# Another written order for the first layer and the seam, late weight tiles inside the loop, and the planes of x at a step's end

## The chip, the cores and the metric

The kernel runs on one core of a Trainium2 chip. A core has a matrix engine (TensorE, PE in the profile), three engines for elementwise work (VectorE, DVE; ScalarE, ACT; GpSimd, POOL) and SyncE (SP), which here issues DMAs. Each engine works through its own instructions in order. The metric is the device time of one execution in microseconds; lower is better.

## The reference

Three parts one behind the other: an attention with gates and a running state over 768 steps (2 batches, 8 heads, width 40), and two layers that multiply 1536 tokens of 320 values by gated weights of 1536 columns.

```python
def _attn_ref(q, k, v, i_gate, f_gate, o_gate):
...
    for t in range(S):
...
        m_new = np.maximum(f_gate[:, :, t] + m, i_gate[:, :, t])
        f_stab = np.exp(f_gate[:, :, t] + m - m_new)
        i_stab = np.exp(i_gate[:, :, t] - m_new)
...
        C = f_stab[:, :, None, None] * C + i_stab[:, :, None, None] * np.einsum('bhd,bhe->bhde', vt, kt)
        n = f_stab[:, :, None] * n + i_stab[:, :, None] * kt
        h_tilde = np.einsum('bhde,bhe->bhd', C, qt)
...
        y[:, :, t] = o * h_tilde / denom

def _moe_ref(x, w_gate, w_val, w_out):
    gate = 1.0 / (1.0 + np.exp(-(x @ w_gate)))
    val = x @ w_val
    return (gate * val @ w_out).astype(np.float32)

def _moe2_ref(x, w_gate, w_val, w_out, rms_g):
    rms = np.sqrt(np.mean(x * x, axis=-1, keepdims=True) + 1e-06)
    xn = x / rms * rms_g
    g = xn @ w_gate
    silu = g * (1.0 / (1.0 + np.exp(-g)))
    val = xn @ w_val
    return (silu * val @ w_out).astype(np.float32)
```

## The kernel before

**Numbers.** Everything is fp32. A product of two fp32 operands is made from planes: each operand is split into a rounded high plane and the low rest (`sub`, L138, makes the low plane; `copy`, L245, the high one). A product of x with the weights is a pass of eight matmuls into one PSUM bank (`ORD`), one with `w_out` is three matmuls. Weights come from HBM as tiles f = 0 to b (12 for each layer), 960 KB each, as 64-bit words from which `top_w` (L201, L203) and `mant_w` (L208) join the halves of the fp32 numbers.

**PLAN.** All of the attention, layer 1, the weights of layer 2 and the first five steps of layer 2 are operations with short names. `op(key, fn)` stores each; a written list, `PLAN`, is run through key by key, and each key issues its instructions on whatever engines it uses. `pin` then ties every engine, SP among them, to exactly this order. So a key sets its place on each of its engines, and an instruction that waits holds all those behind it on its engine. The keys, with c a chunk of 256 tokens, f a tile:

- D, E: matmuls on nothing, for an idle TensorE; Fb, F, P, S, K, V, PV, U, I, H, A, O: attention (F is a scan on VectorE, S a product of q and k); X: the result goes to `xT`, transposed, high (XH) and low (XL) plane.
- LW, WT, WM, WO, WG, WR, WL..: load and planes of a layer 1 tile; T, TS, TH, Y: one chunk and tile of layer 1. The last two chunks go together (Tp, Sp, Mp, Hp, Yp).
- LZ (load), ZT (top half: ScalarE for even f, VectorE for odd f), ZM (joined halves), ZG, ZR, ZO (high planes), ZLG, ZLH, ZLR, ZLS, ZOL (low planes): a tile of layer 2. Near the end of PLAN the loads share one buffer: the next one can be issued when the ZM of the last has read it.
- N: the norm. RW, RD, RJ, RH, RL: the first third of x for layer 2: 16-bit planes on GpSimd, a transposing DMA, joined again, high, low.
- Tq (`w_up`, L649; the last digit is the pass), Sq (sigmoid), Mq1 and Mq2 (the two multiplies on VectorE), Hq1 (`fb`, ScalarE), Hq2 (`ft`, GpSimd), Yq (`w_out`, L755): steps 0 to 4 of layer 2. `Mq42` is the second multiply of step 4.

**The loop.** Steps 5 to 35 of layer 2 (12 tiles for each of three groups of 512 tokens) follow in a Python loop. A step i issues, in this order: `r_up(i, 0)`, the second half of `r_out(i-2)`, `r_up(i, 1)` (all matmuls on half the rows, L671, two at a time), sigmoid `w_sg`, multiply `w_m1`, the first half of `r_out(i-1)`, then the work on x for the next group, then `w_m2`, `w_h` (`fb`) and `w_hl` (`ft`). Groups of these matmuls are tied: the first of a group waits for a nop on SP, and that nop waits for the last matmul of the group two before (`behind`, L662). Step 5 has `w_up` in place of `r_up`.

The work on x for the next group is spread over steps by `ev`: four row blocks, one begun per step from step 5 (and 17) on: `d_planes` (GpSimd, two copies, L521, L522), one step later `d_move` (a DMA_TRANSPOSE issued by SP), one later `d_join` (GpSimd, L530) and, at the step's end, `d_h` (ScalarE) and `d_l` (VectorE, which writes the tile the profile calls `wraw`). From the third block on, `d_planes` writes a buffer that a `d_l` has to have read.

Of the kernel before, what the change touches and what calls it, by code (L numbers as in the profile page):

```python
# [51 lines left out]
D0 D1 D2 Lga Gm Gf1 Gi1 Gie D3 Lgr Gf2 Gfe Gmz Gfh Gid Lgs Lqk01 Ltok01 D4 Gt D5 D6 Lqk00 Gse Gms Rm Lms Ltok00 Gfl Gtg O00 O01 Lmr LW0 D7 D8 D9 Fb00
F00 Fb02 D10 Fb03 D11 D12 D13 Fb01 S01 S00 D14 V01 D15 D16 D17 D18 D19 D20 Ri1 K00 F03 F02 F01 P01 Rie V00 PV01 K02 K03 D21 D22 P03 PV03 A01 Rf1 K01
Rf2 U00 Rfe WT0 Lsel P02 P00 H01r H01a Rer H01b LW2 WM0 Rel Rz LW1 Lfd Ltok10 Lqk10 Lf10 Lqg10 Lf11 PV00 WO0 UC00 A03 XR00 UM00 A00 H00r H03r H03a H00a
H00b WT2 Rt2 E0 Rc2 D23 D24 E1 D25 D26 D27 D28 WG0 PV02 XP00 E2 E3 E4 E5 Rg U01 WM2 WO2 LW3 LW4 H03b WR0 WG2 A02 WR2 WLG0 WLG2 H02a H02r WLR2 H02b WLS2
WLR0 WT1 XR01 Rgc UC01 Rt1 Lf12 Rc1 E6 E7 E8 D29 XP01 S10 WM1 WO1 E9 XH01 XH00 XL01 XL00 T02 F10 F11 P10 WLS0 WLH0 T00 Lqg11 Lqk11 Lf13 I10 Ltok11 O10
WG1 WR1 WLR1 TS02 WOH2 TH02 P11 V10 WLG1 K10 WLH1 WLS1 LW5 Lqg20 Lf21 Y020 PV11 LW8 WT3 TS00 WT4 TH00 WM3 IH10 T01 UM01 TS01 WO3 PV10 Y000 Y001 F12 WM4
TH01 H10a Y011 S11 K11 Y021 Y010 WR3 WG3 WLR3 WO4 F13 P13 P12 I11 V11 H10b PV13 PV12 WLG3 WLS3 WLH3 WG4 A10 H10r H10c XR10 WR4 O11 IH11 XP10 H11a A11
XH10 WLH4 WLR4 WOH4 H11r H11b H11c T03 U10 LW9 Lf20 LW6 Lqk20 UC10 WT5 WLS4 WLG4 T04 WO5 TS03 XR11 XP11 TS04 XH11 TH03 XL10 TH040 XL11 WM5 UM10 Y031
I20 Y030 WOH5 WR5 WG5 T11 WOL2 K12 WOL4 F21 TS11 WT8 TH11 T10 TS10 WLH5 K13 WLS5 WLG5 WO8 TH10 WM8 WLR5 T12 Ltok21 Lqg21 WT6 TH041 TH042 LW7 TS12 TH120  # L60
T14 Y040 Y041 WO6 WM6 F20 Y111 Y110 TS14 WG8 TH121 TH122 WR8 T05 WT9 WOH6 WR6 WOH3 WG6 WLR8 TH140 TH141 WOL6 IH20 Y121 Y100 T15 WLH8 WLS8 WLS6 WOL5
WLG6 WLG8 S20 Y101 Lf23 Ltok20 V20 LWa Lf22 Lqk21 LWb TH142 WLH6 K21 TS15 TS05 WT7 TH150 P20 Y120 WO9 TH151 TH050 WLR6 T18 T06 O20 TH051 TH052 TS18 WO7
WM7 P21 U11 UC11 K20 TH152 F22 TH180 F23 PV20 Y140 PV21 Y050 Y141 WG7 TS06 WR7 WLG7 U20 Y151 Y150 T16 Y051 WLS7 WM9 WOH7 TH181 WTa WR9 TH182 UC20 TH060
H20a WTb WOH8 A20 TH061 TS16 TH160 TH161 T13 T08 WLH7 H20r WLR7 WG9 WLG9 K22 WLS9 V21 TH162 Y161 S21 TH062 UM11 TS13 WOL8 WOa Y160 Y180 TH130 WMa WOb
TS08 T07 P23 TH080 WLR9 TH081 I21 T19 TH082 WGa TS07 IH21 WMb WRb P22 TH070 WLGa Y080 Y181 WOL3 WOL7 K23 PV22 Y081 PV23 WGb TH071 WRa WLSa TH072 WLSb
H21a WLRa TS19 TH131 TH132 A21 H21r TH190 Ltok30 Lf31 Lqk30 Lf30 F30 T17 Y061 Y130 T1a Y060 Y070 Y071 S30 Y131 WLGb O21 WOH9 TS17 TH191 WOHa TH192 TS1a
TH170 WOL9 H20b F31 WLRb H21b H21c H20c TH171 WOHb T1b P31 TH172 K30 WOLa WOH0 XR20 WOH1 TH1a0 P30 WOLb TS1b TH1b0 Y191 Y190 XP20 P030 XR21 V30 V030
TH1b1 P031 TH1a1 TH1b2 T09 TH1a2 UM20 Lrms Ltok31 Lf32 Lf40 Lqk31 Lqk41 Lqg30 XP21 T0b Y1b1 F32 P131 XH21 TS09 XH20 XL20 XL21 TH090 Y171 U21 V130 Y1a0
Y1b0 Y170 V230 T23 V31 K31 V330 TS0b TH0b0 P231 N100 TH0b1 O30 TH091 TH0b2 F40 P130 N101 Y1a1 T0a Y0b1 P230 TS23 TH230 TH092 N102 Y090 Y091 Y0b0 UC21
P331 TH231 N110 TS0a WOL0 V031 V131 TH232 UM21 WOL1 TH0a0 P330 TH0a1 TH0a2 N103 T24 PV31 I30 PV30 IH30 H30a N111 N112 N113 A30 Ltok41 T27 U30 Y0a1 Y0a0  # L70
TS24 TH240 UC30 K32 Lf42 S31 TS27 O31 TH241 N000 N010 P32 N011 N012 P032 LZ0 Lf33 ZT0 V231 N001 TH270 F33 T29 T25 P132 P33 H30r TH242 TS25 N013 TH250
N002 P232 TH251 K33 TH252 T20 Y241 Lqg31 T22 Y251 I31 P332 N003 P033 P133 P233 P333 V331 Y230 PV32 Y240 PV33 TS22 IH31 TH220 H30b H30c H31a Lqk40 Lf41
Ltok40 TH271 V40 TH272 F41 K41 Y231 U31 Y250 Y270 Y271 S40 A31 XR30 TH221 K40 H31b TS29 TH290 TH291 UC31 TH292 P40 P41 TS20 P041 Lqg40 Lf43 T28 T21
XP30 V040 P040 H31r P141 TH200 XH30 TH201 H31c V140 TH222 TH202 UM30 XL30 TS28 TH280 TS21 TH210 F42 T2a Y220 Y221 V240 V340 Y200 U40 Y201 UC40 T26 T2b
I40 TH211 P241 P341 P140 TH281 TH212 V41 TH282 P240 TS26 P340 IH40 TH260 Y290 Y291 PV41 PV40 Y210 Y281 XR31 TS2a TH261 TH262 XP31 Y261 V041 V141 TS2b
V241 XH31 UM31 K42 V341 H40a TH2a0 F43 TH2b0 XL31 Y260 Y280 TH2b1 TH2b2 S41 Y211 P43 P42 TH2a1 O40 Lf50 Lqk50 TH2a2 T32 T30 P042 P043 H40b P143 P243
O41 TS30 P142 TS32 P343 Y2b0 Y2b1 Y2a0 Y2a1 T36 Lqg41 I41 Ltok50 Lf51 N200 N210 A40 P242 F51 TH320 TH321 N201 P342 TH300 IH41 Lqg50 K43 UM40 TH322 PV42
PV43 TH301 H41a F50 N211 T31 TH302 V50 A41 TS31 TH310 TH311 TS36 V050 H41r H40r S50 P50 H41b N202 N212 TH312 V150 P51 H40c N203 I50 T38 H41c P051 P050
TH360 T37 Ltok51 Lf52 Lf53 Lqk51 V51 Lqg51 P150 TS37 P250 IH50 P151 N213 T33 Y300 V250 P251 XR41 V350 TH370 Y321 Y301 XP41 Y320 P350 PV50 TH371 TH361
TH362 TH372 TS33 P351 PV51 F52 H50a XH41 V051 F53 A50 H50r TH330 XL41 Y311 T39 Y310 V151 S51 U41 P53 UC41 T3a TS38 TH331 TH332 TS39 V251 XR40 P053 V351  # L80
UM41 P52 XP40 Y331 TH380 TH390 P153 P052 O50 O51 XH40 P152 Y330 T34 H50b XL40 H50c I51 P253 TH381 P353 PV53 P252 P352 PV52 IH51 Y370 Y371 Y361 XW50
TH382 XD50 TH391 TH392 Y360 Y380 Y391 Y381 TS34 H51a H51b A51 H51r H51c XW51 TS3a TH3a0 TH340 TH3a1 XJ50 XH50 TH341 TH3a2 XL50 T35 TS35 TH350 Y3a1 Y390
T3b LZ2 XD51 TH342 XJ51 Y3a0 Y341 Y340 TH351 ZT2 TH352 Y350 TS3b XH51 XL51 ZM0 Tp30 Tp31 TH3b0 TH3b1 TH3b2 Y3b0 N300 Y3b1 Tp00 ZM2 Y351 Sp3 Mp32 Hp31
N310 Sp0 Tp10 RW2 LZ1 RD2 LZ4 ZT4 ZT1 N311 N301 N312 N313 Hp32 ZM1 N302 N303 LZ3 Tp11 Tp01 Tp20 Yp32 Mp02 ZM4 Sp2 Hp01 Hp02 Sp1 Tp21 Tp70 Yp33 Yp02
Yp30 Yp00 Yp01 Yp03 Yp31 RJ2 ZT3 Mp12 Hp11 RH2 ZO0 Mp22 Hp21 ZM3 ZR0 ZG3 RW0 Hp12 Tp71 LZ6 LZb Tp60 Yp13 Yp11 Yp12 Sp7 Mp72 ZTb ZMb Hp22 ZOL0 Yp20 RD0
LZ7 Yp23 Yp21 Yp22 Yp10 Tp50 Tp61 Sp6 ZG0 ZO1 Hp71 ZO3 RJ0 ZLS0 ZLG3 ZOL1 ZOL3 Hp72 ZLH3 Mp62 Tp41 Yp73 ZG1 ZT6 ZR1 RH0 ZO2 ZG2 Sp5 Hp61 ZR2 ZT7 Hp62
Tp90 Tp40 Yp72 Yp71 Tp51 Yp63 Yp61 ZR3 Sp4 ZLR0 ZLR1 ZOL2 ZLG1 ZLG0 Yp60 Yp62 Yp70 ZM6 Mp42 RL2 ZLR2 Mp52 ZLS3 ZLS1 ZLG2 RW1 Tpb0 Tp91 ZM7 ZO6 Hp51
Hp52 ZG7 ZG6 Hp41 Sp9 ZR6 ZR7 ZLS2 ZLG7 Hp42 Mp92 ZLR7 Yp50 Tpb1 Yp41 Yp51 Yp40 Yp52 Yp42 Yp53 Yp43 ZLR6 LZ5 RD1 RL0 ZLR3 Spb ZG4 ZLS6 RJ1 RW3 RD3 RH1
RL1 Mpb2 Tpa0 Hp91 ZO7 Tp80 ZO4 ZOL6 ZLH2 Hp92 ZLG6 ZLS7 Sp8 Hpb1 Hpb2 Spa Tpa1 Tp81 Ypb1 Yp93 Yp91 Mp82 Ypb3 ZT5 Yp92 Yp90 Ypb2 Ypb0 RJ3 RH3 Hp81 ZGb
RL3 ZM5 Mpa2 ZLG4 Tq20 Hpa1 ZO5 ZOb Hp82 LZ8 Tq00 Hpa2 Yp83 Ypa3 ZR4 ZR5 Sq2 N510 ZG5 Sq0 ZT8 Ypa0 Tq01 Ypa2 Yp80 Yp82 Mq21 N511 ZOLb ZOL7 ZLH6 N512  # L90
ZLHb Mq01 N513 Yp81 Tq30 Tq21 Tq10 Ypa1 ZLGb N500 ZLR5 Mq02 N501 N502 N503 Mq22 Hq01 Hq02 Sq3 N400 N401 ZLH7 N402 ZOL5 ZOL4 ZRb N410 N411 N412 Yq02
# [1117 lines left out]
```

## Time and profile before

| | |
|---|---|
| median of 3 runs | 482.18 us (481.48 to 483.06) |
| the profiled execution's own time | 480.16 us |
| its span, first to last instruction | 478.3 us |
| TensorE busy | 457.5 us, 96% |
| VectorE, ScalarE, GpSimd busy | 265.1, 201.0, 232.7 us |
| TensorE's mean granted clock | 0.986 |

The profile's times count from the span's start. In the table, an engine's busy time is the sum over its instructions; what is missing to the span is time in which it waited. Attention and layer 1 fill the first 200 us and overlap with layer 2's first weights behind that; the first matmuls of the loop's tied groups (L671) start at 309.77.

### The profile page before, as it was taken

How to read it: one execution, taken by the hardware profiler on the slowest of the kernel's cores; microseconds unless marked ns; L12 is line 12 of the kernel's file. 1: busy time of each engine (PE TensorE's matmuls, PEld its weight loads, DVE VectorE, ACT ScalarE, POOL GpSimd, SP SyncE). 2: the span in 40 equal slices, each digit the busy share in tenths (PEclk: the TensorE clock that was granted, in tenths of full speed). 3: DMA queues.
4: the chain of work that ended last, by engine and by line, in shares of the span. 5: the costliest groups of instructions: out<-in, count | busy, mean ns of one | idle time of the engine just before them, and what ended most of it. 6: DMA issues, size and time to landing. Idle time of an engine off the chain costs nothing.

```text
span 478.3 us, 9850 instructions
## 1 busy us (share of the span) xinstructions
PE 457.5 (96%) x3915; PEld 411.5 (86%) x3917; DVE 265.1 (55%) x464; ACT 201.0 (42%) x448; POOL 232.7 (49%) x287
## 2 busy tenths in 40 slices
...
GB/s 191 333 325 361 318 172 121 11 148 66 212 39 66 65 147 1 117 198 232 97 100 16 84 1 83 83 20 41 9 57 1 18 34 18 20 38 1 1 1 58
DMA packets 24388, 46.68 MB, mean 98 GB/s; under 512 B 12726, under 2 KB 16198, under 8 KB 24342
## 3 DMA queue, kind: packets, MB, share of 16 engines
...
HBM read 41.24 MB, written 2.05 MB: 90 GB/s over the span
## 4 chain that ended last, share of the span: by engine, by line
PE 87%; DVE 4%; ACT 3%; POOL 2%; DMA 2%; issue 1%; DVEq 0%; ACTq 0%; POOLq 0%; SPq 0%
PE g L597 15%; PE o L671 11%; PE g L671 11%; PE a L671 9%; PE o L630 7%; PE g L649 6%; PE a L649 6%; PE o L755 5%; PE o L597 3%; PE a L340 2%; DMA wraw<-in_w_dram 2%; PE a L432 2%; PE o L627 2%; PE a L430 1%; PE g L602 1%; POOL ft L138 1%
## 5 line engine op out<-in xcount | busy, mean ns | idle before, releaser
L138 POOL TENSOR_TENSOR ft<-p,fb 128x512 fp32r<-128x512 f32 x47 | 61.4, 1308 | 114.2 <-ACT fb L245 113.4
L597 PE MATMUL g<-xT,w 128*128 128x256 f32 x640 | 84.1, 286 | 0.6 <-DVE xT L138 0.6
L597 PEld LDWEIGHTS g<-xT,w 128*128 128x128 f32 x640 | 79.5, 191 | 1.4 <-DVE xT L138 0.8
L671 PE MATMUL a<-xT,w 64*128 64x512 f32 (+1 forms) x310 | 79.8, 385 | 0.0
L671 PE MATMUL g<-xT,w 64*128 64x512 f32 (+1 forms) x310 | 79.8, 385 | 0.0
L239 DVE TENSOR_TENSOR p<-p,g 128x512 f32<-128x512 f32 (+1 forms) x37 | 24.9, 673 | 98.3 <-ACT p L728 96.2
L671 PE MATMUL o<-w,fb 64*128 64x320 f32 (+1 forms) x508 | 57.9, 308 | 12.2 <-ACT fb L245 12.2
L728 ACT ACTIVATE p<-g 128x512 f32<-128x512 f32 x47 | 28.0, 596 | 83.1 <-PE g L671 64.6
L671 PEld LDWEIGHTS o<-w,fb 64*128 64x128 f32 (+1 forms) x508 | 45.5, 187 | 17.3 <-ACT fb L245 12.7
L671 PEld LDWEIGHTS g<-xT,w 64*128 64x128 f32 x310 | 55.0, 187 | 4.0
L671 PEld LDWEIGHTS a<-xT,w 64*128 64x128 f32 x310 | 55.0, 187 | 3.8
L245 ACT ACTIVATE fb<-p 128x512 fp32r<-128x512 f32 (+1 forms) x49 | 30.4, 620 | 58.7 <-DVE p L239 50.8
L138 POOL TENSOR_TENSOR h<-sig,h 128x256 fp32r<-128x256 f32 x42 | 36.2, 866 | 36.4 <-ACT h L245 35.5
L239 DVE TENSOR_TENSOR p<-p,a 128x512 f32<-128x512 f32 (+1 forms) x49 | 33.0, 676 | 27.6 <-ACT p L728 14.7
L630 PE MATMUL o<-w,h 128*128 128x320 f32 x252 | 46.4, 318 | 0.0
L671 PE MATMUL a<-wraw,w 64*128 64x512 f32 (+1 forms) x155 | 44.0, 379 | 0.0
L671 PE MATMUL g<-wraw,w 64*128 64x512 f32 (+1 forms) x155 | 44.0, 379 | 0.0
L671 PE MATMUL o<-w,ft 64*128 64x320 f32 (+1 forms) x254 | 40.5, 313 | 1.9 <-POOL ft L138 1.9
L630 PEld LDWEIGHTS o<-w,h 128*128 128x128 f32 x252 | 37.6, 189 | 1.1 <-POOL h L138 0.5
L138 POOL TENSOR_TENSOR w<-wc,w 128x256 fp32r<-128x256 f32 (+2 forms) x37 | 25.2, 685 | 13.7 <-ACT w L245 8.9
L671 PEld LDWEIGHTS g<-wraw,w 64*128 64x128 f32 x155 | 28.3, 185 | 3.5
L671 PEld LDWEIGHTS a<-wraw,w 64*128 64x128 f32 x155 | 28.3, 185 | 2.3
...
## 6 DMA issues: line engine op xcount, KB each, us to landing
wraw<-in_w_dram SPq DMA_DIRECT2D x24, 959.8 KB, 6.3
...
```

What stands on the lines that cost most here:

```text
L138: eng.tensor_tensor(out=out, in0=a, in1=b, op=ALU.subtract)
L239: eng.tensor_tensor(out=out, in0=a, in1=b, op=op)
L245: a_.activation(out=out, in_=x, func=AF.Copy, scale=scale)
L340: nc.tensor.matmul(out=st[j][:, i * L:(i + 1) * L], lhsT=t[n, 1, i, :], rhs=t[n, 0, i, :], start=True, stop=True)
L432: nc.tensor.matmul(out=ps[:, (o + i) * E:(o + i + 1) * E], lhsT=p[:, i, :], rhs=w[:, o + i, :], start=True, stop=True)
L597: nc.tensor.matmul(out=g[:, m, :], lhsT=w[:, m, ws, :], rhs=x[xs // 3][:, xs % 3, :], start=(i == 0), stop=(i == 7))
L627: nc.tensor.matmul(out=o, lhsT=h[:, b * L:(b + 1) * L], rhs=o32[f], start=(n == 1), stop=(n == NF))
L630: nc.tensor.matmul(out=o, lhsT=h[:, hs, b * L:(b + 1) * L], rhs=wo_t[f][:, ws, :], start=(n == 1 and i == 0), stop=(n == NF and i == 2))
L649: nc.tensor.matmul(out=g, lhsT=w[:, m, ws, :], rhs=x[xs // 3][:, xs % 3, :], start=(i == 0), stop=(i == 7))
L671: k = nc.tensor.matmul(**kw).ins
L728: a_.activation(out=s, in_=keep["w", k, f, 0], func=AF.Sigmoid)
L755: nc.tensor.matmul(out=o_ps[key][:, 0:DM], lhsT=h[hs][:, n], rhs=wo_t[f][:, ws, :], start=(c == 1 and i == 0), stop=(c == NF and i == 2))
```

## The change

There are three edits. (1) `PLAN` is another permutation of its keys. (2) `LATE`, empty before, names nine keys of weight tile a of layer 2 (all but its load); they are no longer in `PLAN`, and the code that was there already issues them at the end of step 5. (3) `d_planes` is called at the end of a step, no longer ahead of `store` and `w_m2`. Every count of operations stays. One line fewer in `PLAN` makes all later line numbers of the changed kernel one or more lower.

```diff
 PLAN = """
...
-ZLS5 Yq13 Yq11 Yq10 Yq32 ZM8 ZO8 ZG8 ZR8 LZa ZLG8 ZOL8 ZLR8 ZLS8 Sq4 ZTa ZMa ZRa ZLRa LZ9 ZT9 Mq41 ZOa ZOLa ZLSa ZM9 ZG9 ZO9 ZR9 ZLH9 ZLR9 ZLS9 ZLG9
-ZOL9 ZGa ZLGa Yq33 Yq31 Yq12 Mq42 Hq41 Hq42
...
+LZ9 ZRb ZGb ZLSb Hq32 ZLH6 ZLRb ZT9 ZM9 Sq4 Yq30 Yq12 Yq31 Mq41 Mq42 Hq41 Hq42 Yq32 Yq33 ZO9 ZR9 ZG9 ZLG8 LZa ZLH7 ZLGb ZLS9 ZLHb ZLH9 ZLR9 ZOL9 ZLG9
 """
...
-LATE = ""
+LATE = "ZTa ZMa ZGa ZRa ZOa ZLGa ZLSa ZLRa ZOLa"
...
         if x[2]:
             d_join(x[2][0])
-        if x[0]:
-            d_planes(x[0][0], x[0][3])
         store()
         w_m2(k, f)
         w_h(k, f)
...
             d_h(*x[2][:3])
             d_l(*x[2][:3])
+        if x[0]:
+            d_planes(x[0][0], x[0][3])
         if i == NP:
             for key in LATE.split():
                 part.pop(key)()
```

Three places follow as each engine sees them, before and after.

VectorE at the end of PLAN, before: low planes of tile 8 (`w_3747`), the joined halves of tile a (`raw_3761`), the top half and the joined halves of tile 9 (`top1_83<-wraw_3767`, `tok_3774`), and step 4 of layer 2 (`p_3758`: with `g` it is Mq41, with `a` Mq42).

```order
L138 TENSOR_TENSOR w_3747<-wc_3745,w_3747 128x2x256
L138 TENSOR_TENSOR w_3747<-wc_3745,w_3747 128x320
L138 TENSOR_TENSOR w_3747<-wc_3745,w_3747 64x128
L208 SCALAR_TENSOR_TENSOR raw_3761<-wraw_3752,top0_82 128x960
L138 TENSOR_TENSOR w_3763<-raw_3761,w_3763 64x128
L203 CAST top1_83<-wraw_3767 128x960
L239 TENSOR_TENSOR p_3758<-p_3758,g_3719 128x512
L208 SCALAR_TENSOR_TENSOR tok_3774<-wraw_3767,top1_83 128x960
L138 TENSOR_TENSOR w_3776<-tok_3774,w_3776 64x128
L138 TENSOR_TENSOR w_3776<-tok_3774,w_3776 128x320
L138 TENSOR_TENSOR w_3763<-raw_3761,w_3763 128x2x256
L239 TENSOR_TENSOR p_3758<-p_3758,a_3710 128x512
```

The same place after: `wraw_3639` and `wc_3703` are tile b, `wraw_3739` and `tok_3749` tile 9, `p_3651` the multiplies of step 3, and `p_3751` those of step 4.

```order
L202 CAST top0_82<-wraw_3639 128x960
L238 TENSOR_TENSOR p_3651<-p_3651,g_3612 128x512
L207 SCALAR_TENSOR_TENSOR wc_3703<-wraw_3639,top0_82 128x960
L238 TENSOR_TENSOR p_3651<-p_3651,a_3653 128x512
L137 TENSOR_TENSOR w_3706<-wc_3703,w_3706 128x320
L137 TENSOR_TENSOR w_3706<-wc_3703,w_3706 64x128
L202 CAST top1_83<-wraw_3739 128x960
L207 SCALAR_TENSOR_TENSOR tok_3749<-wraw_3739,top1_83 128x960
L238 TENSOR_TENSOR p_3751<-p_3751,g_3712 128x512
L238 TENSOR_TENSOR p_3751<-p_3751,a_3730 128x512
L137 TENSOR_TENSOR w_3627<-wc_3569,w_3627 128x2x256
L137 TENSOR_TENSOR w_3774<-tok_3749,w_3774 64x128
```

What moved: tile a is gone from here (its joined halves now come behind step 5's multiplies), and both multiplies of step 4 stand together behind tile 9, ahead of the last low planes of tiles 8 and 9.

GpSimd at the start of the loop, before: `ft` of the steps from 4 on among the copies of `d_planes` (`xw<-xn`) and `d_join` (`xw<-xw`).

```order
L138 TENSOR_TENSOR ft_3799<-p_3758,fb_3798 128x512
L521 COPY xw_3835<-xn_2347 128x2x320
L522 COPY xw_3835<-xn_2347 128x2x64
L138 TENSOR_TENSOR ft_3840<-p_3820,fb_3839 128x512
L521 COPY xw_3906<-xn_2350 128x2x320
L522 COPY xw_3906<-xn_2350 128x2x64
L138 TENSOR_TENSOR ft_3911<-p_3889,fb_3910 128x512
L530 COPY xw_3835<-xw_3835 128x2x384
L521 COPY xw_3979<-xn_2952 128x2x320
L522 COPY xw_3979<-xn_2952 128x2x64
L138 TENSOR_TENSOR ft_3984<-p_3961,fb_3983 128x512
```

The same place after, from step 5's `ft` on; `w_3834` are planes of tile a, out of LATE.

```order
L137 TENSOR_TENSOR ft_3825<-p_3808,fb_3824 128x512
L520 COPY xw_3828<-xn_2362 128x2x320
L521 COPY xw_3828<-xn_2362 128x2x64
L137 TENSOR_TENSOR w_3834<-raw_3832,w_3834 64x128
L137 TENSOR_TENSOR w_3834<-raw_3832,w_3834 128x320
L137 TENSOR_TENSOR ft_3908<-p_3889,fb_3907 128x512
L520 COPY xw_3911<-xn_2344 128x2x320
L521 COPY xw_3911<-xn_2344 128x2x64
L529 COPY xw_3828<-xw_3828 128x2x384
L137 TENSOR_TENSOR ft_3981<-p_3961,fb_3980 128x512
L520 COPY xw_3988<-xn_2994 128x2x320
```

What moved: the copies of a step now stand behind its `ft`, and tile a's planes ahead of the second `ft` shown.

VectorE shortly ahead of layer 1's first product, before: weight planes (`w`, `wc`, `o32`) among the scaling of the attention's result (`x`, `r`), then the two low planes of the first `xT`, then the first scan of chunk 1 (L242).

```order
L138 TENSOR_TENSOR w_356<-wc_345,w_356 128x2x256
L239 TENSOR_TENSOR x_155<-x_155,a_326 128x160
L461 RECIPROCAL r_358<-r_358 128x4
L138 TENSOR_TENSOR w_356<-wc_345,w_356 64x128
L465 SCALAR_TENSOR_TENSOR x_155<-r_358,x_155 128x160
L138 TENSOR_TENSOR w_324<-wc_271,w_324 64x128
L208 SCALAR_TENSOR_TENSOR wc_400<-wraw_275,top0_82 128x640
L208 SCALAR_TENSOR_TENSOR o32_402<-wraw_275,top0_82 128x320
L138 TENSOR_TENSOR xT_405<-o1_386,xT_405 128x3x128
L138 TENSOR_TENSOR xT_405<-o0_331,xT_405 128x3x128
L242 SCALAR_TENSOR_TENSOR ft_427<-early_278,ident4_74 128x512
```

The same place after.

```order
L460 RECIPROCAL r_321<-r_321 128x4
L464 SCALAR_TENSOR_TENSOR x_232<-r_321,x_232 128x160
L137 TENSOR_TENSOR w_296<-wc_276,w_296 64x128
L137 TENSOR_TENSOR xT_336<-o0_327,xT_336 128x3x128
L137 TENSOR_TENSOR xT_336<-o1_365,xT_336 128x3x128
L241 SCALAR_TENSOR_TENSOR ft_379<-fb_356,ident4_74 128x512
L137 TENSOR_TENSOR w_340<-wc_306,w_340 64x128
L137 TENSOR_TENSOR w_340<-wc_306,w_340 128x2x256
L207 SCALAR_TENSOR_TENSOR wc_383<-wraw_354,top0_82 128x640
L207 SCALAR_TENSOR_TENSOR o32_385<-wraw_354,top0_82 128x320
L241 SCALAR_TENSOR_TENSOR ft_420<-early_358,ident4_74 128x512
```

What moved: the low planes of `xT` and one scan now stand ahead of four operations on weights (`w_340` twice, `wc_383`, `o32_385`).

## Rows read from the trace of the kernel before

**Rows 1.** The page, engines: busy us (share of the span) xinstructions.

```profile
PE 457.5 (96%) x3915; PEld 411.5 (86%) x3917; DVE 265.1 (55%) x464; ACT 201.0 (42%) x448; POOL 232.7 (49%) x287
```

**Rows 2.** TensorE's waits: who for whom, us in total, times, longest.

```profile
PE o L671 <- ACT fb L245: 12.2, 1, 12.2
PE o L671 <- POOL ft L138: 1.9, 3, 0.7
...
PE g L597 <- DVE xT L138: 0.6, 1, 0.6
```

**Rows 3.** Stretches: length, busy PE PEld DVE ACT POOL, PEclk, DMA, GB/s.

```profile
10.00:200.00 190.00, 188.77 (x1685) 178.63 (x1686) 152.20 (x291) 104.06 (x258) 114.34 (x156) 1.00 0.50 159
160.00:190.00 30.00, 30.00 (x303) 29.33 (x302) 27.43 (x55) 16.47 (x45) 14.42 (x20) 1.00 0.27 85
190.00:297.50 107.50, 107.43 (x603) 94.80 (x602) 54.73 (x88) 49.28 (x107) 62.15 (x72) 1.00 0.34 103
...
297.50:309.80 12.30, 0.05 (x3) 0.03 (x2) 5.69 (x9) 3.92 (x10) 3.90 (x6) 0.63 0.24 81
309.80:317.70 7.90, 7.45 (x56) 6.20 (x58) 1.38 (x2) 1.03 (x2) 4.33 (x6) 0.71 0.02 5
```

**Rows 4.** The chain of waits, 283 to 316: start us, us, what.

```profile
283.69 2.05 PE o L755 x14
...
291.12 4.60 DMA wraw<-in_w_dram
...
297.07 1.17 DVE raw L208
...
298.26 4.72 DMA wraw<-in_w_dram
...
303.00 0.71 DVE top L203
...
309.09 0.64 ACT fb L245
```

**Rows 5.** Timeline of TensorE: start, us, what, [idle before <-releaser].

```profile
295.55 1.30 PE L649 MATMUL a<-xT,w 128*128 128x512 f32 x5
...
309.77 0.90 PE L671 MATMUL o<-w,fb 64*128 64x320 f32 x4 [12.25 <-ACT fb L245]
...
317.64 0.45 PE L671 MATMUL o<-w,fb 64*128 64x320 f32 x4
...
322.83 0.45 PE L671 MATMUL o<-w,fb 64*128 64x320 f32 x4
...
329.21 0.41 PE L671 MATMUL o<-w,ft 64*128 64x320 f32 x2 [0.74 <-POOL ft L138]
```

**Rows 6.** The page's DMA issues: KB each, median us to landing.

```profile
wraw<-in_w_dram SPq DMA_DIRECT2D x24, 959.8 KB, 6.3
```

**Rows 7.** Timeline of GpSimd, in the loop.

```profile
326.96 0.72 POOL L521 COPY xw<-xn 128x640 uint16<-128x640 uint16 x1 [3.82 <-DVE wraw L138]
...
327.88 1.27 POOL L138 TENSOR_TENSOR ft<-p,fb 128x512 fp32r<-128x512 f32 x1
...
400.62 1.29 POOL L138 TENSOR_TENSOR ft<-p,fb 128x512 fp32r<-128x512 f32 x1 [2.00 <-ACT fb L245]
```

**Rows 8.** Timeline of ScalarE, in the loop.

```profile
325.26 0.63 ACT L245 ACTIVATE fb<-p 128x512 fp32r<-128x512 f32 x1 [1.55 <-DVE p L239]
```

**Rows 9.** Timeline of SP's queue, in the loop.

```profile
327.94 1.21 SPq L526 DMA_TRANSPOSE xw<-xw  x1
```

**Rows 10.** Timeline of VectorE, at four places.

```profile
25.90 1.04 DVE L208 SCALAR_TENSOR_TENSOR o<-wraw,top 128x320 int32<-128x320 int32 x1
...
289.64 1.40 DVE L208 SCALAR_TENSOR_TENSOR wc<-wraw,top 128x960 int32<-128x960 int32 x1 [3.31 <-POOL w L138]
...
326.34 0.56 DVE L138 TENSOR_TENSOR wraw<-xw,xT 128x384 fp32r<-128x384 f32 x1 [1.11 <-ACT xT L245]
...
400.98 1.34 DVE L138 TENSOR_TENSOR wraw<-xw,xT 128x384 fp32r<-128x384 f32 x1 [1.11 <-ACT xT L245]
```

More of the change, by code (lines that the diff above doesn't have):

```diff
@@ L51 @@
 PLAN = """
[L52 to L91, printed above, removed]
@@ L92 @@
-Hq21 Hq22 Mq31 Sq1 N413 ZLR4 ZLG5 N403 ZLS4 Tq11 Tq31 Yq03 Yq01 Yq23 Yq21 Yq00 Yq20 Yq22 Mq32 ZLRb Mq11 Mq12 Hq31 Hq32 Hq11 Hq12 Tq41 Tq40 Yq30 ZLSb
-ZLS5 Yq13 Yq11 Yq10 Yq32 ZM8 ZO8 ZG8 ZR8 LZa ZLG8 ZOL8 ZLR8 ZLS8 Sq4 ZTa ZMa ZRa ZLRa LZ9 ZT9 Mq41 ZOa ZOLa ZLSa ZM9 ZG9 ZO9 ZR9 ZLH9 ZLR9 ZLS9 ZLG9
-ZOL9 ZGa ZLGa Yq33 Yq31 Yq12 Mq42 Hq41 Hq42
+Lga Gm Gf1 Gf2 Gfe Gmz Gfh D0 D1 D2 D3 D4 D5 D6 D7 D8 D9 D10 Lgs Lgr Gms Gi1 Rm Gie Gfl Gse Fb02 Gid F02 D11 Lqk00 Lqk01 Ltok01 Fb01 D12 Gt D13 D14 F01
+Lms Fb03 D15 D16 D17 D18 D19 Gtg Fb00 Ltok00 Lmr K02 V01 Rf1 Ri1 Rf2 Rfe Rie F03 F00 S00 S01 P01 V00 LW0 O00 O01 P03 P02 P00 K01 K00 K03 D20 D21 D22
@@ new lines @@
+D23 PV01 A01 Lsel WT0 PV03 U00 H01a H01r Rer H01b Rz Rel LW2 WO0 WM0 UC00 A03 XR00 PV00 A00 UM00 WT2 WR0 WG0 H03a H00a H00r H00b H03r H03b WM2 WO2 D24
+D25 D26 D27 E0 PV02 A02 WLS0 H02a H02r H02b XP00 WLG0 WLH0 Rg Rgc XH00 XR01 WR2 E1 E2 U01 WLS2 Lqk10 Lfd LW1 Lf11 Lqg10 Lf10 Ltok10 Rt1 D28 XP01 XH01
+WT1 Rc1 WLR0 XL00 XL01 Rt2 Rc2 WG2 F11 WLR2 WLG2 WM1 WO1 D29 E3 E4 E5 E6 E7 E8 T00 S10 F10 WG1 WR1 P10 P11 LW3 Lf12 T02 Ltok11 Lf13 Lqk11 V10 I10 K10
+WLG1 WLH1 WLS1 TS02 TS00 WLR1 TH02 IH10 TH00 PV11 PV10 UC01 WT3 F12 K11 H10a WM3 WO3 T01 Y001 E9 Y000 Y021 S11 Y020 LW4 O10 TS01 WR3 A10 O11 Lqg11 H10b
@@ new lines @@
+TH01 WLR3 F13 V11 P13 UM01 WG3 WT4 H10r P12 H10c Y010 PV13 I11 PV12 Y011 LW5 WM4 WO4 XR10 WG4 WR4 LW8 IH11 H11a H11b A11 H11r H11c XP10 WLR4 XH10 WT5
+XL10 WLG3 WLH3 WLS3 T03 U10 XR11 TS03 Lf21 Ltok20 WLH4 WLG4 WLS4 LW6 LWb LW9 XP11 XH11 TH03 T04 WT8 WM5 WO5 XL11 TS04 Lqk20 V20 WO8 K12 TH040 T11 WOH4
+TS11 TH041 K13 WOL4 T14 UC10 WM8 WG8 TH11 T10 WR8 TH042 WLG8 WLS8 WG5 WR5 TS14 WLH5 WLG5 U11 Y041 Y030 Y031 WOH8 WT6 WLH8 TH140 WOL8 WLR8 T12 Lqg20 LW7
+WLR5 UC11 Y110 Y040 Y111 TH141 WOH2 TS12 WLS5 TH142 TH120 WOH5 TH121 TS10 WM6 TH10 F21 WO6 TH122 T15 T08 S20 WOH3 WOL2 Y101 Y121 Lqk21 WT7 WG6 WR6 TS08
```

31 lines of the change are left out of this document (added).

## The prediction

> **What bounds the kernel now.** I read the page first. TensorE is busy for 457.5 of 478.3 us, so the time is TensorE's own work plus about 21 us in which it stands still [rows 1]. The order changes but no matmul is added or dropped, so the change can only give back those 21 us, or add to them, or move TensorE's clock.
>
> Next the list of what TensorE waits for. One wait is more than half of the 21 us: 12.2 us for the copy `fb` on ScalarE. Three waits for `ft` on GpSimd make 1.9, one for the lower plane of `xT` on VectorE 0.6 [rows 2]. The table by stretches places the long one: from 297.50 to 309.80 TensorE does 0.05 us of work. It also shows a price behind it: from 309.80 to 317.70 the granted clock is 0.71, against 1.00 from 190 to 297.50. Elsewhere there is little to find: 190 to 297.5 has 107.43 us of work in 107.50, 10 to 200 has 188.77 in 190 [rows 3].
>
> Then the chain of waits, for why `fb` is late. Before `fb` (309.09) there stand, one behind the other: a weight load of 4.60 us, ScalarE's cast of it, VectorE's join of halves of 1.17, a second load of 4.72, and a cast of 0.71 [rows 4]. These are tiles a and 9 of layer 2: `LZa ZTa ZMa LZ9 ZT9`. The `fb` awaited is that of step 4 of layer 2 (`Hq41`), which needs neither tile. It waits because VectorE and ScalarE work in the written order, and `Mq41` and `Mq42` are written behind those tiles.
>
> **The stall at the seam between PLAN and loop.** Its price is the wait, 12.25, and the slow step behind it: the `fb` halves of `r_out` start at 309.77, 317.64 and 322.83, so one step took 7.87 us and the next 5.19, which is 2.68 more [rows 5]. Together 14.93 us.
>
> Does the new order remove it? I walked the new PLAN from the start of `Tq20` (t = 0) with durations of before. On TensorE a pass of eight matmuls takes 8/5 of 1.13 us (295.55 to 296.68), 1.81, and a `Y` of three 3/14 of 2.05, 0.44 [rows 4, 5]. From `Tq20` to the end of step 5's `w_up` there are 12 passes and 24 Ys: 32.4 us. Then `fb` is wanted.
>
> VectorE and ScalarE: `Tq01` ends at 3 passes and 4 Ys, 7.2. Behind `Mq01` and `Mq02` comes `ZM8`, done at 9.7, which frees a buffer for load b: 4.72 brings 14.4. `ZTb` stands behind `Mq12`, which needs `Tq10` (6 passes and 8 Ys: 14.4), its sigmoid and two multiplies: `ZTb` is done at 17.1, `Mq31` at 17.8, `ZMb` at 19.0. Load 9 lands at 23.8; `ZT9` (0.71) and `ZM9` (1.17) bring 25.9 with their starts, the two multiplies 27.4, `fb` (0.64) 28.1, `ft` 29.4. So `fb` has 4.3 us to spare, and `ft` (wanted a little later) about 3.5. I count the whole 14.93.
>
> Where does tile a go? Its load can start behind `ZM9`, 25.9, and lands at 30.7. `ZTa` now stands behind step 5's `fb` on ScalarE (about 33.9), so the load no longer holds anything. `ZTa`, `ZMa` and three copies end about 38, when step 6's sigmoid becomes wanted. I cost it at nothing: that step's `ft` is wanted only one step of 5.19 us behind the end of its matmuls, and needs 4.4. Without that cover the price would be the join that stands in front, 1.17, and its cast, about as long.
>
> The loads at this place took 4.60 and 4.72; the median to landing of all 24 is 6.3 us [rows 6], and with it the two would take 3.2 of the 4.3 us. The Trainium skill, "DMA: Bandwidth & Descriptors", the section on the anatomy of one DMA, gives a fixed part plus bytes over a rate, for another kind of queue: about 4.25 us for such a load (an estimate from that page). By it 5.2 us would be to spare and the first rival below would have little chance; the rows at the seam are nearer to it than the median is, and the sum is the same by all three as long as something is to spare.
>
> **The planes.** `d_planes` copies a row block of x on GpSimd. In before it stands ahead of the step's `ft` and has to wait for the buffer that `d_l` reads: 3.82 us idle, then 0.92 of copies, and `ft` starts at 327.88 [rows 7], where its `fb` was done at 325.89 [rows 8]. That costs TensorE 0.74 at 329.21 [rows 5], twice in the kernel (two row groups get their planes in the loop; the third `ft` wait, 0.45, is in the 2.68). Moved behind `ft`: −1.48.
>
> What is late next? The step's up matmuls end at about 322.83 [rows 5], `fb` 3.06 later; with 1.27 of `ft` that is 4.4, and with 1.0 of copies the planes now end 5.4 us behind the up matmuls. The DMA transpose reads them, and its issue takes SP 1.21 us [rows 9]. Behind it on SP stands the nop that the next step's first matmul waits for. So that matmul can start at 5.4 + 1.21 + a little = 6.65, where the step's rhythm wants it at 6.07 (an `r_out` half, six pairs at 2.05/14 us, and a step of 5.19). That is 0.6 us. Once a step has slipped, the next transpose is in time, so it hits about every second one of four per group.
>
> There is a second effect. `d_l` took 0.56 us at 326.34, with GpSimd idle, and 1.34 at 400.98, where it met the `ft` of 1.29 that had started at 400.62 [rows 7, 10]: it ended 0.41 behind that `ft`. In after every `d_l` meets an `ft` in this way, and the third and fourth planes wait for a `d_l`: +0.35 there. Per group 0.6 + 0.6 + 0.35, for both groups +3.1. Bounds: 0, if the issue does not hold SP's nops, and 5.0, if all eight places pay 0.63. I take 3.1, as the 1.21 is SP's own row.
>
> The Trainium skill speaks against the move here: "SBUF — State Buffer", the section on its two separate sides, says that a VectorE instruction with two SBUF inputs and a GpSimd instruction shut each other out for a whole instruction. By that rule `d_l` would start only at the end of `ft` and end 0.56 behind it instead of the measured 0.41, which makes the sum 0.3 higher.
>
> **The start.** VectorE now writes the lower planes of the first `xT` before four operations on weights that stood ahead; one of these alone is 1.04 us [rows 10], more than the 0.6 that TensorE waited [rows 2]. I take −0.6. More can't come from it; the bound on the other side is such a wait behind the first scans, which other operations now precede, +0.6.
>
> **The body of layer 1.** The same operations in another turn. It was nearly free of waits, so it can hardly get better; one new wait of the size of the longest there, 0.6, is my value (0.7 with its edges), six of them the upper bound: 0 to +4.
>
> **Sum.** 480.16 (the profiled execution: a span of 478.3 and 1.86 around it) − 14.93 − 1.48 + 3.1 − 0.6 + 0.7 = 466.95. The runs' median, 482.18, lies 2.02 above that execution: **469.0 us**.
>
> **Rivals.**
> - *Part of the stall stays* (the change doing less than it says). Tile 9 is not in LATE; `ZT9` and `ZM9` still stand ahead of `Mq41`. With both loads at 6.3 instead of 4.72, 3.2 of the 4.3 are gone; if `ZMb` also waits for its buffer as `ZM8` did, 3.31 [rows 10], `fb` comes 2.2 late and TensorE slows for a part of a step (half of 2.2): 472.3. For it: that wait and the median; against: the 4.60 and 4.72 of just these loads. 12%.
> - *New waits in layer 1.* The new order was not walked wait by wait there, and loads, scans and weight tiles meet elsewhere. Six to ten waits of 0.6: 472 to 475. For it: VectorE works 27.43 of 30 us between 160 and 190 [rows 3]. 8%.
> - *Slower.* The same place gone over its edge: VectorE bound. Between 10 and 200 it idles for 37.8 of 190 us, in 160 to 190 for 2.57 of 30. One operation written ahead of its load stops everything behind it; once the stops in such a stretch exceed the 2.57 us, each further one is TensorE's. They must reach 2.6 + 15 to take the gain back and lose 1.5 more: 484. Against it: no load of before makes TensorE wait there. 6%.
> - *Better.* SP's transposes hold nothing (−3.1) and layer 1 has no new wait (−0.7): 465.2. For it: no row of before shows an SP nop behind a waiting transpose. 10%.
> - The forecast, 64%. Its own range is 465.5 to 472.5.
>
> **Range and chances.** 464.8 to 475.0 leaves out the slower rival, the upper end of the layer 1 one, and some of the forecast's tails. A difference of 0.3% is 1.5 us, about what a measurement can tell here. Slower is the slower rival, 0.06; same, 0.03, the layer 1 one at three times its size; faster the rest, 0.91.
>
> **What would show it.** In the profile of the changed kernel: no wait for `fb` at L670 above 1 us, and a granted clock of 1.00 across the seam; no `ft` wait of 0.74, but waits of some 0.3 to 0.9 of the up matmuls at L670, two or three in each row group, with a DMA_TRANSPOSE of SP just ahead; `d_l` at 1.3 to 1.4 us; no wait at the first `T`. The prediction is wrong if `Mq42` again stands behind a load at the seam, if layer 1's stretch has several us of TensorE waits, or if those SP holds are absent.

## The result, and the profile after

The changed kernel took 468.61 us, median of 4 runs (468.03 to 469.60); the kernel before, in the same runs, 481.96. The ratio is 0.9722, 95% interval 0.9698 to 0.9746: faster by 13.4 us. The profiled execution took 468.03 us with a span of 466.2, against 480.16 and 478.3.

First TensorE's waits after, in the columns of [rows 2], complete.

```profile
PE g L670 <- SPq L661: 3.5, 5, 1.4
PE o L1010 <- POOL gates L1001: 1.3, 1, 1.3
PE g L670 <- DVE p L238: 0.6, 1, 0.6
PE a L406 <- DMA early<-in_qg_dram: 0.6, 1, 0.6
PE a L502 <- DVE xT L137: 0.5, 1, 0.5
```

The 12.2 us for `fb` and the three waits for `ft` are gone. In their place the first up matmul of a step waits behind SP, 3.5 us in five places. (L661 is the nop on SP. The 0.6 put down to DVE is a sixth such place, as the SP row below shows.) The two waits at L406 and L502 lie in the start, at 40.15 and 45.77; before there were three there, from 13.44 to 27.93.

The table by stretches, columns of [rows 3].

```profile
280.00:297.50 17.50, 17.50 (x101) 15.48 (x101) 13.18 (x17) 6.98 (x16) 10.20 (x12) 1.00 0.33 114
297.50:309.80 12.30, 10.90 (x114) 9.88 (x110) 5.34 (x7) 5.16 (x9) 9.92 (x13) 1.00 0.08 17
```

The stretch in which TensorE did 0.05 us of work [rows 3] now has 10.90, and the granted clock stays at 1.00.

VectorE at the seam, in order of time.

```profile
289.49 1.29 DVE L202 CAST top<-wraw 128x960 f16<-128x960 bf16 x1 [1.78 <-DMA wraw<-in_w_dram]
290.81 1.16 DVE L207 SCALAR_TENSOR_TENSOR tok<-wraw,top 128x960 int32<-128x960 int32 x1
291.89 0.68 DVE L238 TENSOR_TENSOR p<-p,g 128x512 f32<-128x512 f32 x1
292.67 0.69 DVE L238 TENSOR_TENSOR p<-p,a 128x512 f32<-128x512 f32 x1
...
299.89 2.29 DVE L207 SCALAR_TENSOR_TENSOR raw<-wraw,top 128x960 int32<-128x960 int32 x1 [1.96 <-ACT top L200]
```

ScalarE there.

```profile
293.45 0.63 ACT L244 ACTIVATE fb<-p 128x512 fp32r<-128x512 f32 x1 [4.77 <-DVE p L238]
```

Tile 9's cast, its joined halves and both multiplies of step 4 run without a gap, and `fb` is done at 294.08. Tile a's join comes at 299.89, out of the way of step 4, but beside the first planes, as shown below. TensorE, with the places of its waits in the loop:

```profile
296.70 0.56 PE L670 MATMUL o<-w,fb 64*128 64x320 f32 x4
...
304.44 0.47 PE L670 MATMUL g<-xT,w 64*128 64x512 f32 x1 [1.40 <-SPq L661]
...
310.23 0.46 PE L670 MATMUL g<-xT,w 64*128 64x512 f32 x1 [0.32 <-SPq L661]
...
316.15 0.47 PE L670 MATMUL g<-xT,w 64*128 64x512 f32 x1 [0.45 <-SPq L661]
...
321.95 0.47 PE L670 MATMUL g<-xT,w 64*128 64x512 f32 x1 [0.30 <-SPq L661]
...
369.54 0.47 PE L670 MATMUL g<-xT,w 64*128 64x512 f32 x1 [0.61 <-DVE p L238]
...
381.24 0.46 PE L670 MATMUL g<-xT,w 64*128 64x512 f32 x1 [1.05 <-SPq L661]
```

`fb` is wanted at 296.70, so it had 2.6 us to spare. The chain of waits of after shows what stands ahead of 310.23.

```profile
306.61 1.28 POOL ft L137
307.90 0.66 POOL xw L520
308.56 0.23 POOL xw L521
308.79 1.02 POOL xw L529
309.81 0.22 SPq L525
310.16 0.07 issue
310.23 0.46 PE g L670
```

`ft`, then the copies of the planes, then SP's transpose, then the matmul. SP's queue, at two of the other places:

```profile
303.02 1.23 SPq L525 DMA_TRANSPOSE xw<-xw  x1
...
368.10 1.24 SPq L525 DMA_TRANSPOSE xw<-xw  x1
```

Each ends about 0.2 us ahead of the matmul that waited (304.44, 369.54). This is the hold that was forecast. GpSimd shows what goes with the longest, the first: the planes of step 5 took 1.67 where 0.72 is usual, beside tile a's join of 2.29 above. Without these 0.95 the hold of 1.40 would be 0.45 (an estimate), about as long as the next three.

```profile
299.86 1.31 POOL L137 TENSOR_TENSOR ft<-p,fb 128x512 fp32r<-128x512 f32 x1
301.09 1.67 POOL L520 COPY xw<-xn 128x640 uint16<-128x640 uint16 x1
302.70 0.29 POOL L521 COPY xw<-xn 128x128 uint16<-128x128 uint16 x1
```

Tile a's late work also stands ahead of step 6's sigmoid (L727) on ScalarE:

```profile
302.22 1.66 ACT L244 ACTIVATE w<-raw 128x512 fp32r<-128x512 f32 x4 [2.42 <-DVE raw L207]
303.78 0.58 ACT L727 ACTIVATE p<-g 128x512 f32<-128x512 f32 x1
```

Step 6's up matmuls had given way to `r_out` at 302.00. In a step without tile a the sigmoid starts 0.3 behind that point (362.65 and 362.96), here 1.8. The `ft` of 306.61 in the chain above follows at 4.6 instead of 3.2 (365.88), 1.4 late.

To count the loop without its start, I took the start of the first up matmul of each step in the timeline of TensorE and subtracted. Most steps come out at 5.18 to 5.20. The table gives, in us, what each step takes above 5.19: for the steps from 6 on (group 1) and for those from 18 or 20 on that take more (group 2).

```
kernel            group 1                       group 2                    r_out of step 5 at
before            0.98 0.00 0.99 0.02           0.99 0.02                  309.77 (waited 12.25)
after             1.57 0.60 0.73 0.61 0.08      0.82 0.08 1.24 0.08        296.70
```

Before's first 0.98 is the end of the slow clock and its two 0.99 are the `ft` waits of 0.74. After has 3.6 and 2.2, from the SP holds. The seam, from the end of step 5's matmuls to the first up matmul of step 6, took 14.83 (297.52 to 312.35) and now 0.98 (296.70 to 297.68).

### The profile page after: what moved, and what is told of

Read it like the earlier page. It is cut to its first block, busy times and chain, and to the rows that moved or that the text cites. A ratio compares the mean times of both kernels' runs of the same rounds, so it can differ in the third digit from the quotient of the medians.

```text
span 466.2 us, 9858 instructions
## 1 busy us (share of the span) xinstructions
PE 455.9 (98%) x3917; PEld 426.9 (92%) x3917; DVE 267.4 (57%) x464; ACT 200.0 (43%) x446; POOL 231.7 (50%) x287
## 4 chain that ended last, share of the span: by engine, by line
PE 82%; DVE 6%; DMA 6%; ACT 2%; POOL 2%; issue 1%; SPq 0%; DVEq 0%; ACTq 0%; POOLq 0%
PE g L596 15%; PE g L670 10%; PE o L670 10%; PE a L670 9%; PE o L629 8%; PE a L648 5%; PE g L648 5%; PE o L754 5%; DMA wraw<-in_w_dram 4%; PE o L596 3%; PE a L339 2%; DVE p L238 2%; PE a L429 1%; PE g L601 1%; DMA early<-fd 1%
## 5 line engine op out<-in xcount | busy, mean ns | idle before, releaser
L727 ACT ACTIVATE p<-g 128x512 f32<-128x512 f32 x47 | 27.9, 596 | 77.2 <-PE g L670 63.8
L670 PE MATMUL o<-w,fb 64*128 64x320 f32 (+1 forms) x508 | 60.9, 305 | 0.0
L670 PEld LDWEIGHTS g<-xT,w 64*128 64x128 f32 x310 | 54.0, 185 | 5.9 <-DVE p L238 2.1
L670 PEld LDWEIGHTS o<-w,fb 64*128 64x128 f32 (+1 forms) x508 | 54.6, 184 | 0.8 <-issue 0.5
L137 POOL TENSOR_TENSOR h<-sig,h 128x256 fp32r<-128x256 f32 x42 | 33.5, 802 | 41.5 <-ACT h L244 40.4
L670 PE MATMUL o<-w,ft 64*128 64x320 f32 (+1 forms) x254 | 47.4, 308 | 0.0
L137 POOL TENSOR_TENSOR w<-wc,w 128x256 fp32r<-128x256 f32 (+2 forms) x37 | 26.6, 725 | 10.9 <-ACT w L244 8.1
L670 PEld LDWEIGHTS o<-w,ft 64*128 64x128 f32 (+1 forms) x254 | 31.7, 184 | 0.0
```

Source lines behind the costliest of these rows:

```text
L137: eng.tensor_tensor(out=out, in0=a, in1=b, op=ALU.subtract)
L670: k = nc.tensor.matmul(**kw).ins
L727: a_.activation(out=s, in_=keep["w", k, f, 0], func=AF.Sigmoid)
```

## The experiments

Each ran beside the kernel before on the same chip; ratios are to it. In the first four that kernel took 480.73 us, in the last four 481.31.

**The planes alone.** The kernel before with only `d_planes` at the step's end.

```diff
-        if x[0]:
-            d_planes(x[0][0], x[0][3])
         store()
...
             d_l(*x[2][:3])
+        if x[0]:
+            d_planes(x[0][0], x[0][3])
```

> The kernel before with one part of the change: d_planes at the end of a step; PLAN and LATE as before. Theory (the planes' copies end later, SP's DMA_TRANSPOSE holds the nop of the next step's first group): the two ft waits of 0.74 go, holds of about 0.6, 0.35 and 0.6 us come in each of the two row groups, together -1.5 + 3.1 = +1.6 us, about 483.5, ratio 1.003; the 12.2 us wait for fb stays. Rival (the move is a gain by itself and the holds of the changed kernel come from its other order): -1.5 us, ratio 0.997, and no wait of the up matmuls behind SP.

483.69 us, ratio 1.0063 (1.0045 to 1.0081): 0.6% slower, about twice the expected size. TensorE's waits in the loop, timeline:

```profile
326.56 0.46 PE L671 MATMUL g<-xT,w 64*128 64x512 f32 x1 [0.61 <-DVE p L239]
...
332.22 0.47 PE L671 MATMUL g<-xT,w 64*128 64x512 f32 x1 [0.21 <-SPq L662]
...
338.28 0.47 PE L671 MATMUL g<-xT,w 64*128 64x512 f32 x1 [0.60 <-DVE p L239]
...
385.84 0.46 PE L671 MATMUL g<-xT,w 64*128 64x512 f32 x1 [0.60 <-DVE p L239]
...
397.56 0.46 PE L671 MATMUL g<-xT,w 64*128 64x512 f32 x1 [1.06 <-SPq L662]
```

The listed waits come to 0.61 + 0.21 + 0.60 + 0.60 + 1.06 = 3.08, where 3.1 was forecast, and the waits of 0.74 for `ft` are gone; three lie in the first group and two in the second, not three in each. The steps lost more than these waits: from step 7 on they took 0.77, 0.47, 0.87, 0.09 above 5.19, and from step 18 on 0.78, 0.08, 1.26, 0.10, together 4.4, where the two steps of before took 1.98. That is +2.4. Step 6, behind the stall, took 1.67 above 5.19 instead of 0.98; the granted clock behind the stall was 0.67 for 9.6 us (311.0 to 320.6), where before had 0.71 for 7.9 [rows 3]. Together the loop is 3.1 longer, about the measured 3.0. (This execution was the slowest of its six and also came 1.4 later to the seam.) So the move of the planes, by itself, is a loss. The rival falls.

**The planes back.** The changed kernel with `d_planes` at its old place: the diff above, turned round.

> The changed kernel with d_planes back at its old place. Theory: the SP holds (1.40, 0.32, 0.45, 0.30, 0.61, 1.05: 4.1 us) go and two ft waits of 0.74 return, -2.6 us: about 466.0, ratio to before 0.967. Rival (the new order and the move belong together, step 5 needs its ft ahead of the copies): 468.6 or more, with new ft waits at steps 5 and 6.

465.65 us, ratio 0.9701 (0.9670 to 0.9731). Against the changed kernel's 0.9722 and 0.9737 (below) the intervals overlap, so the time alone doesn't separate the two. The trace does: no wait behind SP is left, and the waits for `ft` are

```profile
303.16 0.41 PE L670 MATMUL o<-w,ft 64*128 64x320 f32 x2 [0.31 <-POOL ft L137]
...
314.55 0.41 PE L670 MATMUL o<-w,ft 64*128 64x320 f32 x2 [0.74 <-POOL ft L137]
...
377.80 0.41 PE L670 MATMUL o<-w,ft 64*128 64x320 f32 x2 [0.74 <-POOL ft L137]
```

The loop's steps took 2.6 above 5.19 (0.60, 0.01, 1.00, then 1.00), the changed kernel's 5.8: 3.2 less. The rival is half right: a new `ft` wait stands at the first step, but of 0.31.

**The transpose issued later.** In the changed kernel, only the place on SP's queue moves.

```diff
             r_up(k, f, 0)
+            if ev.get((1, i - 1)):
+                d_move(ev[1, i - 1][0])
             r_out(*seq[i - 2], split[i - 2][1])
...
-        if x[1]:
-            d_move(x[1][0])
```

> The changed kernel, only the issue of the DMA_TRANSPOSE moves: behind the first up group of the next step instead of ahead of its nop. Planes, copies and joins stay. Theory (it is SP's queue that holds the matmuls): the waits of the up matmuls behind SP go, -4.1 us, about 464.5, ratio to before 0.964; no new wait, as the next nop is wanted 1.8 us later and the issue takes 1.2. Rival (the up matmuls wait for something else that ends at the same time, the copies on GpSimd or the sigmoid): waits of the same size stay under another name, 468.6.

463.89 us, ratio 0.9649 (0.9627 to 0.9671), clear of the changed kernel's interval: the fastest version tried, and faster than both kernels. Its list of waits has none in the loop; the table by stretches:

```profile
297.00:330.00 33.00, 32.96 (x342) 29.07 (x342) 17.12 (x20) 11.74 (x21) 21.10 (x25) 1.00 0.13 26
```

The changed kernel has 30.54 of 33.00 there. The transposes take SP as long as before, beside matmuls that run:

```profile
303.32 1.23 SPq L525 DMA_TRANSPOSE xw<-xw  x1
```

So it was SP's queue that held the matmuls, and not the copies or the transpose itself. One step still took 0.32 too long (5.51), the others 5.19.

**LATE alone.** The kernel before, with tile a's nine keys in LATE and its load behind tile 9.

```diff
-... ZR8 LZa ZLG8 ... Sq4 ZTa ZMa ZRa ZLRa LZ9 ZT9 Mq41 ZOa ZOLa ZLSa ZM9 ZG9 ... ZOL9 ZGa ZLGa Yq33 ...
+... ZR8 ZLG8 ... Sq4 LZ9 ZT9 Mq41 ZM9 LZa ZG9 ... ZOL9 Yq33 ...
-LATE = ""
+LATE = "ZTa ZMa ZGa ZRa ZOa ZLGa ZLSa ZLRa ZOLa"
```

> The kernel before with LATE's nine keys of tile a taken out of PLAN and issued at the end of step 5, and tile a's load behind tile 9's ZM; d_planes and the rest of PLAN as before. Theory (the stall at the seam is tile a's load, cast and join ahead of tile 9, and the copies behind them): the wait of 12.2 shrinks to some 3 us, as tile 9's load can start at 291.1 instead of 298.3, and TensorE is slow for less than a step: about 471, ratio 0.977. Rival (the gain sits in the whole order, tile 9 and the buffers keep the wait): the wait stays at 8 us or more, 478. If the rest of the new order is worth nothing, this kernel and the changed one with d_planes back differ only by what is left of this wait.

472.48 us, ratio 0.9827 (0.9807 to 0.9847). The long wait is 4.43 us instead of 12.25:

```profile
301.85 0.90 PE L629 MATMUL o<-w,fb 64*128 64x320 f32 x4 [4.43 <-ACT fb L203]
```

Tile a was 7.8 of the 12.2. The size was missed by a half: VectorE shows what was left out of the count, tile 9's low planes and their wait for ScalarE, still ahead of the multiply.

```profile
289.54 1.41 DVE L166 SCALAR_TENSOR_TENSOR wc<-wraw,top 128x960 int32<-128x960 int32 x1 [3.31 <-POOL w L96]
...
297.15 1.14 DVE L166 SCALAR_TENSOR_TENSOR tok<-wraw,top 128x960 int32<-128x960 int32 x1
299.55 0.93 DVE L96 TENSOR_TENSOR w<-tok,w 64x128 fp32r<-64x128 f32 x2 [1.25 <-ACT w L203]
300.39 0.68 DVE L197 TENSOR_TENSOR p<-p,a 128x512 f32<-128x512 f32 x1
```

**The changed kernel once more.**

> The changed kernel once more, beside the next three on the same chip: ratio to before 0.972 as in the result.

467.72 us, ratio 0.9737 (0.9709 to 0.9765). One of the six executions took 471.64 with a mean granted clock of 0.993; no trace of it was kept, so whether a part of the stall came back there is open.

**LATE, and the multiply ahead of tile 9's planes.** The edit of "LATE alone", and besides:

```diff
-... Mq41 ZM9 LZa ZG9 ZO9 ZR9 ... Yq12 Mq42 Hq41 Hq42
+... Mq41 ZM9 Mq42 Hq41 Hq42 LZa ZG9 ZO9 ZR9 ... Yq12
```

> The kernel before with LATE out of PLAN, as in the run before, and besides step 4's second multiply, fb and ft directly behind tile 9's ZM, ahead of tile 9's copies and low planes. Theory (the 4.4 us that stayed there are two things: tile 9's planes ahead of Mq42, about 2.1, and ZM8's late start behind GpSimd, about 2.3): the multiply ends near 299.0, fb near 299.7, so the wait is 2.2 instead of 4.4, and ft follows at 301.0: about 2 us faster than that run, ratio 0.978. Rival (the copies on ScalarE or the loads set it, not the order behind ZM9): 4.4 stays, 0.983.

470.83 us, ratio 0.9780 (0.9762 to 0.9799), as expected:

```profile
299.13 0.56 PE L629 MATMUL o<-w,fb 64*128 64x320 f32 x4 [2.01 <-ACT fb L203]
```

The 12.25 of the seam are thus 7.8 for tile a, 2.4 for tile 9's planes ahead of the multiply, and 2.0 that remain. These remain with `ZM8` starting at 289.24 behind GpSimd, as it did in before; that this late start causes them was not tried by itself.

**LATE's keys in PLAN.** The changed kernel with its nine late keys as PLAN's last ones.

```diff
 ... ZLR9 ZOL9 ZLG9
+ZTa ZMa ZGa ZRa ZOa ZLGa ZLSa ZLRa ZOLa
...
-LATE = "ZTa ZMa ZGa ZRa ZOa ZLGa ZLSa ZLRa ZOLa"
+LATE = ""
```

> The changed kernel with LATE empty: its nine keys stand as PLAN's last ones, ahead of step 5 instead of behind it. Theory (tile a's load must not stand ahead of a sigmoid): the load issued at 292.0 lands near 296.8, ScalarE's cast, VectorE's join and the copies end near 301, and step 5's sigmoid, now behind them, comes some 5 us late; its fb is wanted at 302.0 and comes near 303.5, ft near 305, the planes behind it later too: +2.5 us, ratio 0.977, with a wait for fb or ft of 1.5 to 2.5 in step 5 or 6. Rival (only the order at PLAN's end matters, LATE is worth nothing): 0.972.

474.67 us, ratio 0.9857 (0.9822 to 0.9893): 7 us slower than the changed kernel beside it, where 2.5 were expected. Between the two profiled executions, 4.6 of it lie in the steps from 6 to 10, and 2.2 ahead of the end of step 5's matmuls, where TensorE's order is the same; the cause of these 2.2 is open.

```profile
305.55 0.56 PE L671 MATMUL o<-w,fb 64*128 64x320 f32 x4 [1.57 <-ACT fb L245]
...
306.91 0.63 PE L671 MATMUL o<-w,ft 64*128 64x320 f32 x2 [0.79 <-POOL ft L138]
...
309.20 0.76 PE L671 MATMUL g<-xT,w 64*128 64x512 f32 x1 [0.86 <-SPq L662]
```

The first wait has the expected size. What was left out is that TensorE waits for `ft` and for the transpose in its wake, and that the granted clock falls: 0.78 between 300 and 312, 0.91 from there to 320.

**The first planes early.** In the changed kernel, the first of a group's four blocks keeps the old place.

```diff
+        if x[0] and not x[0][0][1] % 4:
+            d_planes(x[0][0], x[0][3])
         store()
...
-        if x[0]:
+        if x[0] and x[0][0][1] % 4:
             d_planes(x[0][0], x[0][3])
```

> The changed kernel, the planes of the first block of each row group at their old place (ahead of ft), those of the other three at the step's end. Theory (the longest SP hold, 1.40 at step 7, is long because these copies ran beside tile a's join, 1.67 instead of 0.72): the planes of step 5 are done before that join starts, the first step's extra 1.6 us goes, the next three steps lose about 0.8, 0.5 and 0.9 as in the run that moves the planes alone; -1.4 us in the first group, nothing in the second: ratio 0.969. Rival (every first transpose of a group pays, whatever runs beside): the hold only moves to the next step with its size, 0.972.

469.93 us, ratio 0.9764 (0.9739 to 0.9789): no gain; the interval overlaps the changed kernel's. As a way to get time back the theory falls. The hold of the first step goes, but the copies still ran beside tile a's join (the second copy took 1.22 instead of 0.29), TensorE waited 0.30 for the `ft` behind them, and the next hold is 0.78. The steps from 6 on took 0.58, 0.95, 0.30, 1.04 and 0.09 above 5.19, together 3.0, against 3.3 in the changed kernel run beside it. So this run doesn't separate what the join costs the planes from what the planes' place costs.

## Why the prediction was right, point by point

- **The seam, −14.93.** It went as argued: with the wait gone and the clock at 1.00, the seam is 13.85 shorter and the step behind it (before's first 0.98) has no slow clock any more: 14.83. The walk's 12 passes and 24 Ys add up to 32.3, not 32.4, and took 32.5. The spare time of `fb` was 2.6 us and not 4.3, since tile 9's load went out at 284.66, some 1.3 later than walked, and its cast took 1.29 instead of 0.71. (GpSimd had begun a subtract of 0.74 at 289.46, just ahead of that cast; beside the one of 0.71 it was idle.) The first rival (part of the stall stays) was nearer than its 12% say, but did not happen in the traces of the changed kernel. The experiments on LATE show that neither part does it alone: LATE without the new order leaves a wait of 4.4, and the new order with these keys back at PLAN's end, the one place tried, waits 1.57 for `fb` and is 7 us slower.
- **The planes, −1.48 + 3.1.** The mechanism was right: the `ft` waits went, SP's transposes hold the first matmul of steps. The size was too small. The steps lost 5.8 instead of 3.1, and before's two `ft` waits had cost 1.98 instead of 1.48: net +3.8, not +1.6. The second group goes as forecast, with a hold in every second step (18 and 20), but costs 2.2 instead of 1.55. There the planes ended 5.43 behind the up matmuls and the transpose's issue 6.69 (walked: 5.4 and 6.6), but the matmul started only at 6.89, not 6.65: 0.2 behind the end of the issue, which the walk took as next to nothing. `d_l` went as the row had it: started at 318.15 beside an `ft` that ran from 317.79 to 319.09, it took 1.34 and ended 0.40 behind. The Trainium skill's rule ("SBUF — State Buffer", the section on its two separate sides), by which it would end 0.56 behind, has the effect right and 0.16 too much.
- **Tile a, cost at nothing.** The first group has a hold in all four steps and costs 3.6, 1.4 more than the second. Tile a's late work is what the first group meets besides: the prediction asked only whether a step's `ft` would be late for its own matmuls, but tile a's join met the first planes, and its copies made the next sigmoid, and so the next planes, late. Where tile a is not in the loop (the run with the planes alone), the two groups cost 2.2 and 2.2. No run takes tile a out of the changed kernel's loop without bringing a stall back, so its 1.4 is read from these rows and not shown by itself.
- **Start and layer 1, −0.6 + 0.7.** Step 5's matmuls ended at 296.70 instead of 297.52: −0.8 instead of +0.1. The waits there were 1.1 us before (0.6, 0.3, 0.2) and are 1.1 after (0.6, 0.5), so they don't explain it. In the four traces with the old order this end lies at 297.1 to 298.9, in five with the new one at 296.3 to 297.3, and in the sixth (LATE's keys in PLAN) at 298.5. The ranges overlap, so whether the order made the 0.8 stays open.
- **The sum** was 466.95 for the profiled execution, measured 468.03. The planes' term was 2.2 too small, start and layer 1 together 0.9 too large, the seam 0.1 too large, and 0.3 came off elsewhere. That the sum came within 1.1 us is thus in part luck: its errors had opposite signs.
- The slower rival (VectorE bound in layer 1) did not come about: TensorE waits for nothing between 46 and 300 us. The better one, SP holding nothing, was wrong for this kernel; the kernel with the later transpose is what it described.
